# Decode attention with grouped queries: where SyncE waits for the stores of the output rows

## The chip, the cores and the metric

The kernel runs on one core of a Trainium2 chip. A core has five engines with an instruction queue each: TensorE (PE; its weight loads are listed as PEld), VectorE (DVE), ScalarE (ACT), GpSimd (POOL) and SyncE (SP), and 16 DMA engines. The engines run on their own and meet only through semaphores: an instruction may wait until a semaphore has a value and may change it when it is done. A DMA raises its semaphore by 16 in all when its data has landed. The metric is the device time of one execution, in microseconds (us); lower is better.

## What is computed

One query position attends to 65,536 keys. There are 32 query heads of 128 elements and 8 heads of keys and values, each shared by four query heads. All inputs and the output are bf16.

```
B, Hq, Hkv, Sq, Sk, D = 1, 32, 8, 1, 65536, 128

k = jnp.repeat(k, Hq // Hkv, axis=1)
v = jnp.repeat(v, Hq // Hkv, axis=1)
scores = jnp.einsum("bhqd,bhkd->bhqk", q, k) * D ** -0.5
p = softmax(scores, axis=-1)
out = jnp.einsum("bhqk,bhkd->bhqd", p, v)
```

The output is 32 rows of 128 elements, 8 KB. K and V together are 268 MB, and every element is read once.

## The kernel before

The work is cut into 16 pairs of units (two pairs for each of the 8 heads of keys). For each pair SyncE loads a part of K and of V (`load_k`, `load_v`), TensorE transposes K in blocks of 128 rows into PSUM (`trb`), VectorE and ScalarE copy the blocks to SBUF (`ktb`), and TensorE multiplies them by the four queries of the head. VectorE takes the largest score of each partition, GpSimd the largest over the partitions, ScalarE the exponentials with their sums, and TensorE multiplies the exponentials (`pts`) by V. VectorE keeps the running sum (`acc`), rescaled whenever the maximum grows.

Each engine has a function of its own (`tensor_engine`, `vector_engine`, `scalar_engine`, `gpsimd_engine`, `sync_engine`) that writes its instruction queue by hand; loops are loops on the engine. The order within a queue is the order of the source.

What stands around the change is the end of the program:

- VectorE finishes the first 28 of the 32 output rows while the last values are still being multiplied (`orow`, L378), and ScalarE stores them (L425). The last four rows, those of the last head, come last: TensorE's last products go into `acc` (L309), TensorE transposes `acc` (L208), VectorE divides by the sum of the exponentials (`olast`, L389), and SyncE stores them (L509).
- Both stores raise the same semaphore, `o_sem`, by 16 each. SyncE, whose queue ends with the second store, waits for 32 (L512).
- The five functions are given to a block (L514 to L519). When the block ends, each engine branches to its end, and there all five meet: SyncE, ScalarE, TensorE and VectorE each execute a DRAIN that raises a gather semaphore; GpSimd waits until it has four, and raises a release semaphore by four; the other four each wait for one (EVENT_SEMAPHORE) and take it. In the profile these instructions have line L520, the statement that closes the block.
- SyncE's wait for `o_sem` is not an instruction of its own in the built program: it stands on SyncE's branch to the block's end, which the profile shows as a COMPARE_BRANCH of L520.

The block at the program's start has a meeting of the same kind (L533).

Of the kernel before, what the change touches and what calls it, by code (L numbers as in the profile page):

```python
# [41 lines left out]
def take(e, sem, n=1):  # L42

    e.wait_ge(sem, n)
    e.sem_inc(sem, -n)  # L45


def bass_standalone__gqa_softmax__decode_kernel(nc, q, k, v, out):
# [14 lines left out]
    def row_tile(odd, x):  # L63
        return (x + C) % (2 * T) if odd else x
# [4 lines left out]
    S = es.enter_context  # L69
# [4 lines left out]
    def sem(name):  # L74
        return S(nc.semaphore(name))
# [48 lines left out]
    q_sem, o_sem, s_x, t_z, t_id, t_if, t_qT = (  # L124
        sem(n) for n in ("q_sem", "o_sem", "s_x", "t_z", "t_id", "t_if", "t_qT"))
# [317 lines left out]
    def pairs(x):  # L443

        return x.rearrange("h (c p t) d -> (h c) p (t d)", c=HALVES, p=P)

    def sync_engine(e):
        kp, vp = pairs(kf), pairs(vf)

        def cols(a, b):  # L450
            return slice(a * D, b * D)

        def load_k(i, odd, split=(0,)):

            for n, f in enumerate(split):
                last = (split + (len(K_PARTS),))[n + 1]
                a, b = K_PARTS[f], (K_PARTS + (2 * T,))[last]
                r = row_tile(odd, a) if b - a < 2 * T else 0
                t = r if odd else C + r
                e.dma_start(kbuf[:, cols(t, t + b - a)], kp[i][:, cols(r, r + b - a)]).then_inc(krdy[f], 16)  # L460
                for x in range(f + 1, last):
                    e.sem_inc(krdy[x], 16)

        def load_v(i, ready, a, b):
            e.dma_start(vbuf[:, cols(a, b)], vp[i][:, cols(a, b)]).then_inc(ready, 16)

        def load_both(i, odd):
            take(e, kfree)
            load_k(i, odd)
            take(e, vfree)  # L470
            load_v(i, vrdy[0], 0, 2 * T)
            e.sem_inc(vrdy[1], 16)

        load_k(0, 0, (0, 1, 2))
        load_v(0, vrdy[0], 0, 2 * T)

        for sm in [vrdy[1]] + vpiece:
            e.sem_inc(sm, 16)

        take(e, kfree)  # L480
        load_k(1, 1)
        e.wait_ge(vmid, 1)
        load_v(1, vrdy[0], C, A)
        take(e, vfree)
        e.sem_inc(vpiece[0], -16)
        load_v(1, vrdy[1], A, 2 * T)
        load_v(1, vpiece[0], 0, C)
        with e.Fori(1, H - 1) as h:
            load_both(2 * h, 0)
            load_both(2 * h + 1, 1)  # L490
        i = NR - 2
        take(e, kfree)
        load_k(i, 0, (0, 2))
        take(e, vfree)
        load_v(i, vrdy[0], 0, A)
        load_v(i, vrdy[1], A, 2 * T)
        i = NR - 1
        take(e, kfree)
        load_k(i, 1, (0, 1, 2))
        take(e, vfree)  # L500
        for sm in vpiece:
            e.sem_inc(sm, -16)
        load_v(i, vrdy[0], C, 2 * T)
        e.sem_inc(vrdy[1], 16)
        r = 0
        for n, sm in zip(V_PIECES, vpiece):
            load_v(i, sm, r, r + n)
            r += n
        ins = e.dma_start(of[HR - R:HR, :], olast[:, :])  # L509
        ins.wait_op(t_last, 1, "sem-ge")  # L510
        ins.then_inc(o_sem, 16)
        e.wait_ge(o_sem, 32)  # L512

    block = S(nc.Block())  # L514
    block.tensor(tensor_engine)
    block.vector(vector_engine)
    block.scalar(scalar_engine)
    block.gpsimd(gpsimd_engine)
    block.sync(sync_engine)  # L519
    es.close()  # L520

# [26 lines left out]
```

## Time and profile before

| | |
|---|---|
| median of 3 runs | 629.46 us |
| lowest and highest | 629.41 and 629.58 us |
| the profiled execution's own time | 629.4 us |
| its span, from the first to the last instruction of the program | 627.5 us |
| mean granted TensorE clock | 0.767 |
| HBM read | 268.44 MB, 428 GB/s over the span |

The profile is one execution. Its page lists for each engine the busy time and its share of the span, then the span in 40 slices (a digit is tenths of a slice), the DMA queues, and the chain of work that ended last. Other views list the chain in order of time, the instructions in a window (start, duration, engine, line, operation, output and inputs, and in brackets the idle time before and what ended it), the instructions of one line (durations in ns as least, median and greatest, then the first and last start in us), and who waited for whom (total, times, longest). An engine's name with a q stands for its sequencer: instructions that only wait, branch or issue a DMA, which are not counted as busy. Rows of sequencers are given to 0.1 us in these views; the trace has them in nanoseconds.

### The profile page before, as it was taken

Reading aid. Unit: us, or ns where it says so; the run is one execution under the profiler, and the core shown is the slowest. Engines: PE = TensorE matmul, PEld = TensorE weight load, DVE = VectorE, ACT = ScalarE, POOL = GpSimd, SP = SyncE. Lnnn points to the kernel's source line nnn. Section 1 sums busy time; section 2 is a strip of 40 time slices with the busy share of each in tenths; the row PEclk is TensorE's granted clock in tenths of the full one; section 3 lists DMA queues with packets and bytes.
Section 4 is the critical chain, followed back from the end, with each engine's and each line's share of the span. In section 5 each row is a group of like instructions: output and inputs, shape, how many; then the busy total and the mean of one; then the engine's idle time right before and its main releaser. Section 6 shows DMA issues by size and latency. Waiting matters only on the chain. (4 is left out here: it accounts for less than half of the span.)

```text
span 627.5 us, 26947 instructions
## 1 busy us (share of the span) xinstructions
PE 489.5 (78%) x12290; PEld 484.9 (77%) x12290; DVE 284.5 (45%) x667; ACT 235.4 (38%) x466; POOL 16.4 (3%) x49
## 2 busy tenths in 40 slices
PE   4764995949859597694977949679695894999987
PEld 4664995949859597694977949679695894999886
DVE  4340553616436164451644517245172542747364
ACT  2240442605425154350533605235152451535343
POOL 0000000000000000000000000000000000000000
PEclk9775886959768597795977959678596885969697
DMA  9999999999999999999999999999999999999997
GB/s 378 427 450 402 439 453 418 451 418 451 418 451 418 447 422 439 430 426 439 426 439 430 434 434 430 439 430 439 430 434 434 434 434 430 415 436 429 425 438 303
DMA packets 6443, 268.59 MB, mean 428 GB/s; under 512 B 802, under 2 KB 930, under 8 KB 1186
## 3 DMA queue, kind: packets, MB, share of 16 engines
q1 hardware_dynamic: 6344, 268.44, 99.2%
q8 instruction: 7, 0.11, 0.1%
q10 hardware_dynamic: 90, 0.02, 0.0%
q14 instruction: 2, 0.02, 0.0%
HBM read 268.44 MB, written 0.01 MB: 428 GB/s over the span
## 5 line engine op out<-in xcount | busy, mean ns | idle before, releaser
L139 PE MATMUL trb<-ident,kbuf 128*128 128x128 bf16 x4096 | 302.2, 237 | 108.6 <-PEq L45 102.8
L139 PEld LDWEIGHTS trb<-ident,kbuf 128*128 128x128 bf16 x4096 | 269.9, 107 | 110.3 <-issue 108.0
L233 ACT ACTIVATE ktb<-trb 128x1024 bf16<-128x1024 bf16 x176 | 180.2, 1024 | 350.2 <-PE trb L139 343.7
L235 DVE COPY ktb<-trb 128x1024 bf16<-128x1024 bf16 x336 | 221.7, 688 | 170.2 <-PE trb L139 167.0
L157 PE MATMUL qkb<-qcur,ktb 128*128 128x4 bf16 x4096 | 132.4, 164 | 0.7 <-issue 0.7
L157 PEld LDWEIGHTS qkb<-qcur,ktb 128*128 128x128 bf16 x4096 | 124.6, 96 | 0.8 <-issue 0.8
L183 PE MATMUL pvb<-pts,vbuf 128*128 128x4 bf16 x2560 | 71.7, 166 | 13.4 <-PEq L45 10.0
L183 PEld LDWEIGHTS pvb<-pts,vbuf 128*128 128x128 bf16 x2560 | 69.9, 102 | 15.2 <-issue 14.9
L403 ACT ACTIVATE pts<-qkb,negm 128x160 bf16<-128x160 f32 (+1 forms) x128 | 52.0, 549 | 0.0
L183 PE MATMUL qkb<-pts,vbuf 128*128 128x4 bf16 x1536 | 43.4, 166 | 8.1 <-PEq L45 8.1
L183 PEld LDWEIGHTS qkb<-pts,vbuf 128*128 128x128 bf16 x1536 | 42.4, 104 | 8.7 <-issue 8.6
L270 DVE TENSOR_REDUCE cmax<-qkb 128x4 f32<-128x640 f32 (+1 forms) x32 | 22.1, 691 | 59.0 <-DVEq L45 59.0
L403 ACT ACTIVATION_READ_ACCUMULATOR pts<-qkb,negm 128x1 f32 x128 | 34.2, 268 | 0.0
L439 POOL PARTITION_ALL_REDUCE cmaxa<-cmax x32 | 12.0, 375 | 576.3 <-POOLq L45 576.3
L320 DVE COPY acc<-qkb 128x4 f32<-128x4 f32 x8 | 1.3, 162 | 41.3 <-DVEq L45 41.3
L397 ACT ACTIVATE alpha<-dm 128x4 f32<-128x4 f32 x32 | 6.4, 201 | 32.1 <-ACTq L45 32.1
L298 DVE TENSOR_TENSOR lp<-lp,alpha 128x4 f32<-128x4 f32 x24 | 3.9, 163 | 26.9 <-DVEq L45 26.9
L309 DVE TENSOR_TENSOR acc<-acc,pvb 128x4 f32<-128x4 f32 x32 | 5.0, 157 | 21.0 <-DVEq L45 20.2
L287 DVE TENSOR_TENSOR m<-m,cmaxa 128x4 f32<-128x4 f32 x24 | 3.8, 159 | 8.8 <-DVEq L45 8.8
L306 DVE TENSOR_TENSOR acc<-acc,alpha 128x4 f32<-128x4 f32 x24 | 3.9, 162 | 4.2 <-DVEq L45 3.7
L288 DVE TENSOR_TENSOR dm<-m 128x4 f32<-128x4 f32 x24 | 3.9, 162 | 0.8
L299 DVE TENSOR_TENSOR lp<-lp,rsum 128x4 f32<-128x4 f32 x24 | 3.9, 161 | 0.8
(42 smaller groups left out, 30.1 us busy)
## 6 DMA issues: line engine op xcount, KB each, us to landing
kbuf<-in_k_dram SPq DMA_DIRECT2D x5, 3072.0 KB, 24.2
vbuf<-in_v_dram SPq DMA_DIRECT2D x2, 5120.0 KB, 23.2
vbuf<-in_v_dram SPq DMA_DIRECT2D x3, 3072.0 KB, 19.6
kbuf<-in_k_dram SPq DMA_DIRECT2D x1, 5120.0 KB, 17.4
kbuf<-in_k_dram SPq DMA_DIRECT2D x2, 2048.0 KB, 12.6
vbuf<-in_v_dram SPq DMA_DIRECT2D x1, 2048.0 KB, 18.0
vbuf<-in_v_dram SPq DMA_DIRECT2D x1, 1984.0 KB, 30.9
vbuf<-in_v_dram SPq DMA_DIRECT2D x1, 704.0 KB, 32.2
```

Source lines behind the costliest of these rows:

```text
L139: ins = pe.transpose(trb[j % NTB][:, i * P:(i + 1) * P], kbuf[:, t * D:(t + 1) * D], ident[:, :])
L157: ins = pe.matmul(bank[:, t * R:(t + 1) * R], lhsT=ktb[:, off:off + P], rhs=qcur[:, :], start=True, stop=True)
L183: ins = pe.matmul(vsum[q], lhsT=vbuf[:, r * D:(r + 1) * D], rhs=pts[:, r * R:(r + 1) * R], start=r == a, stop=r == b - 1)
L233: ins = e.activation(dst, trb[j % NTB][:, :], AF.Copy).then_inc(eva, 1)
L235: ins = e.tensor_copy(dst, trb[j % NTB][:, :]).then_inc(evd, 1)
L270: e.tensor_reduce(cmax[:, :], qkb[part][:, 0:n * R].rearrange("p (t g) -> p g t", g=R), AX.X, ALU.max).then_inc(cm, 1)
L288: lambda: e.tensor_tensor(dm[u % 2][:, :], mo[:, :], mn[:, :], ALU.subtract),
L298: chain(e, lambda: e.tensor_tensor(lp[:, :], lp[:, :], alpha[u % 2][:, :], ALU.mult), lambda: e.tensor_tensor(lp[:, :], lp[:, :], rsum[u % ...
L309: return lambda: e.tensor_tensor(acc, acc, vsum[q], ALU.add)
L397: e.activation(alpha[u % 2][:, :], dm[u % 2][:, :], AF.Exp, scale=scale)
L403: ins = e.activation(pv[:, g, r:r + n], sv[:, g, 0:n], AF.Exp, bias=negm[b][:, g:g + 1], scale=scale, accum_out=rsum[b][:, g:g + 1])
L439: e.partition_all_reduce(cmaxa[:, :], cmax[:, :], P, bass.bass_isa.ReduceOp.max).then_inc(cma, 1)
```

## The change

SyncE's wait for `o_sem` is taken out of its function and written behind the block, on SyncE alone. The block is opened and closed by a `with` statement of its own, where before it was closed with the tensors and semaphores by `es.close()`; the meeting's instructions have line L513 in the changed kernel and were L520 in the one before.

```diff
@@ -509,14 +509,15 @@
         ins = e.dma_start(of[HR - R:HR, :], olast[:, :])
         ins.wait_op(t_last, 1, "sem-ge")
         ins.then_inc(o_sem, 16)
-        e.wait_ge(o_sem, 32)
-
-    block = S(nc.Block())
-    block.tensor(tensor_engine)
-    block.vector(vector_engine)
-    block.scalar(scalar_engine)
-    block.gpsimd(gpsimd_engine)
-    block.sync(sync_engine)
+
+    with nc.Block() as block:
+        block.tensor(tensor_engine)
+        block.vector(vector_engine)
+        block.scalar(scalar_engine)
+        block.gpsimd(gpsimd_engine)
+        block.sync(sync_engine)
+
+    nc.sync.wait_ge(o_sem, 32)
     es.close()
```

In the built program, the five queues hold the same instructions in the same order but for two things: SyncE's branch to the block's end carries no wait, and behind SyncE's part of the meeting stands one more instruction, an EVENT_SEMAPHORE that waits for `o_sem` to reach 32 (L520 of the changed kernel). It is the last instruction of SyncE's queue; the other four engines' queues end with the meeting.

## The prediction

> **What bounds the kernel now.** I read the page first, for the span and the engines, then the chain of waits, then the last two microseconds in the timeline, the waits of SyncE, and every instruction of the meeting at the block's end (L520).
>
> ```profile
> span 627.5 us, 26947 instructions
> PE 489.5 (78%) x12290; PEld 484.9 (77%) x12290; DVE 284.5 (45%) x667; ACT 235.4 (38%) x466; POOL 16.4 (3%) x49
> DMA  9999999999999999999999999999999999999997
> q1 hardware_dynamic: 6344, 268.44, 99.2%
> ```
>
> The stream of K and V keeps the 16 DMA engines busy to the last slice (99.2% in q1), and TensorE follows it. The change touches none of this: the instructions that it moves stand after the last load on SyncE's queue. So the question is only what lies between the last store and the end, and that is read from the end of the chain and the timeline:
>
> ```profile
> 624.91 0.17 DVE acc L309
> 625.08 0.04 issue
> 625.12 0.39 PE pvb L208
> 625.50 0.03 issue
> 625.53 0.34 DVE olast L389
> ```
>
> ```profile
> 621.75 0.59 ACTq L425 DMA_DIRECT2D out_dram<-orow  x1
> ...
> 625.53 0.34 DVE L389 TENSOR_SCALAR olast<-pvb,rl 4x128 bf16<-4x128 f32 x1 [0.47 <-PE pvb L208]
> 625.89 0.35 SPq L509 DMA_DIRECT2D out_dram<-olast  x1
> ```
>
> The chain stops at olast; the last 1.6 us hold no engine work at all. They are the issue of the last store (625.89 to 626.24), its flight, and the meeting:
>
> ```profile
> SPq L520 <- DMA out_dram<-olast: 0.8, 1, 0.8
> SPq L520 <- PEq L520: 0.2, 1, 0.2
> ```
>
> ```profile
> L520 POOLq EVENT_SEMAPHORE  x2: 17/17/17, 627.3 to 627.4; - x2
> L520 POOLq DRAIN  x1: 403/403/403, 620.1 to 620.1; - x1
> L520 ACTq DRAIN  x1: 152/152/152, 622.4 to 622.4; - x1
> L520 PEldq DRAIN  x1: 425/425/425, 625.1 to 625.1; - x1
> L520 DVEq DRAIN  x1: 378/378/378, 625.5 to 625.5; - x1
> L520 SPq COMPARE_BRANCH  x1: 38/38/38, 627.1 to 627.1; - x1
> L520 SPq DRAIN  x1: 7/7/7, 627.3 to 627.3; - x1
> L520 SPq EVENT_SEMAPHORE  x1: 17/17/17, 627.4 to 627.4; - x1
> L520 ACTq EVENT_SEMAPHORE  x1: 17/17/17, 627.4 to 627.4; - x1
> L520 DVEq EVENT_SEMAPHORE  x1: 21/21/21, 627.4 to 627.4; - x1
> L520 PEldq EVENT_SEMAPHORE  x1: 51/51/51, 627.4 to 627.4; - x1
> ```
>
> SyncE waits 0.8 us for the store; that wait stands on its branch out of the block (the COMPARE_BRANCH at 627.1). The other engines drained at 620.1 to 625.9 and stand at the meeting. Only then comes SyncE's DRAIN, GpSimd gathers and releases, and all five leave at 627.4. Flight and meeting are in series. The views round these rows to 0.1 us; the trace's records have them in nanoseconds, and they also hold the updates of semaphores, which no view prints. Those that I use, in us from the span's start:
>
> ```
> SP   store L509      625.895 - 626.247
> o_sem reaches 32     627.079
> SP   branch L520     627.096 - 627.134
> SP   DRAIN           627.254 - 627.261
> POOL gather, release 627.286 - 627.303, 627.364 - 627.381
> SP, ACT, DVE, PE leave at 627.423, 627.427, 627.438, 627.469
> o_sem, first store: last update 624.733 (issue L425 ended 622.342)
> unnamed semaphore 2: 627.709 .744 .949 .993 628.016 | .114 .153 .187 .234
> cleared: numbers 207-255 from 628.163 to .254, ..., 3-53 from 628.450 to .799
> unnamed semaphore 2: 629.023 .057 .095 .139 .162 | .260 .299 .333 .379
> ```
>
> The lower half explains why the profiled execution's time is 629.40 and its span 627.47: the 1.93 us are an exit behind the program. One semaphore is passed on nine times, all others are cleared, and it is passed nine times again; the time ends 0.02 us after the last. The second round shows its hops when nobody is late: 34, 38, 44, 23, 98, 39, 34, 46 ns. In the first only the second hop differs (205 for 38): the third engine was late on its own account, by some 0.17 us. Five steps out and four back is a round trip over five engines. The clearing names them: it begins first, and with the fastest steps, in the highest block of numbers, and last, with the slowest, in the lowest. I take the ends for SyncE and TensorE (TensorE's leaving the meeting takes 51 ns, SyncE's 17), so the trip starts at TensorE and turns at SyncE, at 628.016.
>
> The Trainium skill, Runtime: NRT & Kernel Launch, section "The ~15µs preamble/postamble breakdown", describes such an exit: a barrier that goes through the five engines and back, a reset of 51 semaphores by each, a second barrier. Its sizes there (estimates 1.5, 1.5 and 2 us, in sum 5) don't fit the 1.93 us here, so the trace decides them; by either the exit comes after the last engine and its later half is the same before and after.
>
> **The change part by part.** (1) Removed: the wait on the branch. SyncE goes from the store's issue (626.247) to its DRAIN. ACT shows that step with an unconditional branch and no wait: issue L425 ends at 622.342, its DRAIN starts at 622.383, 0.04 us on, and no branch is recorded. So SyncE drains at 626.29. If the branch stays, it costs 38 ns and the 120 ns behind it that the rows above show, and the DRAIN is at 626.45. I take the first, since the branch now has no wait to carry, as ACT's hasn't.
>
> (2) Moved earlier: the meeting. From SyncE's DRAIN to TensorE's leaving it took 627.469 - 627.254 = 0.215 us. It now ends at 626.50 (626.66 with the branch), 0.97 (0.81) earlier. It lies beside the store's flight, 626.25 to 627.08, and nothing of it is on the path. GpSimd, ACT, DVE and PE have no instruction behind the meeting, so nothing of the program is queued for any of them.
>
> (3) Added: one semaphore wait on SyncE alone. It passes where the branch did, 627.096, and takes the 17 ns of SyncE's other EVENT_SEMAPHORE: 627.11. Nothing of the program is queued behind it on SyncE and no DMA is moved past it: the last store keeps its place and its wait for t_last, so 626.247 and the 0.83 us of flight stand. Span after: 627.11, that is 0.36 less.
>
> (4) Behind the span: the exit. TensorE can start the trip at 627.709 - 0.97 = 626.74, and the fourth engine can hand on at 627.993 - 0.97 = 627.02 (627.18 with the branch). SyncE turns it when it is there itself. What it needs between its last instruction and its turn is not visible, since in the profile it was there in time. Bounds: above, 628.016 - 627.423 = 0.59 us, since it was no later than that; below, 0.04, ACT's step from its store to its DRAIN. TensorE, the one engine whose start of the trip waits for no other, needs 627.709 - 627.469 = 0.24. I take 0.24, being the only such step that the trace times directly, and since SyncE's own steps (DRAIN 7 ns, leaving 17) are no slower than TensorE's. The turn is then at 627.11 + 0.24 = 627.35 and not 628.016: 0.66 us less. With 0.59 it is at 627.70, 0.31 less; with 0.04 at 627.15, 0.87 less (0.81 if the branch stays, where the other four decide).
>
> Sum against the profiled execution: 629.40 - 0.66 = 628.74; the median of the runs, 629.46, is 0.06 above it, so 628.80. Of the 0.66, 0.36 is meeting taken out of the span and 0.30 is the other four's way into the exit, which now runs while SyncE waits. The cover is the store's flight: were that nothing, the meeting would be on the path again and the change worth only the branch's 0.16.
>
> **The rivals.** *SyncE is slow into the exit* (0.59 us as the third engine must have been about: 627.381 to 627.949 if that is GpSimd): the gain is 0.31, time 629.15. For it: nothing shows SyncE earlier than 628.016. Against: its steps are the shortest of all.
>
> *The exit doesn't stand on SyncE*, or SyncE is there at once: the whole 0.81 to 0.97 of the meeting comes off, 628.49 to 628.65. Against: a trip over five engines has to pass it.
>
> *The DRAIN waits for the store itself.* Then the change does not do what it says: SyncE drains at 627.08 anyway, the meeting ends 0.215 later, at 627.30, the wait behind passes at once, and only the branch is saved: 629.40 - 0.17 + 0.06 = 629.29. Against it stands ACT: its DRAIN ended at 622.54, with the first store still in its queue:
>
> ```profile
> core 0 of [0], span 627.5 us
> q10 hardware_dynamic: 42, 0.01, 2.0%
> ```
>
> That is the DMA view of 622.54 to 624.5: all 42 packets of the first store move after ACT's DRAIN.
>
> *Slower: the store lands later, because four engines leave while it flies.* Its place is the last store, so far alone on an idle core. The price by the nearest row: the first store, beside the V stream, took 624.733 - 622.342 = 2.39 us against 0.83. With 2.39 the wait passes at 628.65, SyncE turns the trip at 628.89, 0.87 later than before: 630.33. It decides from a flight of 0.83 + 0.66 = 1.49 us on. Against: until SyncE turns the trip the four do no more than four semaphore updates (the clearing began only behind 628.016), and the store's 8 packets were through by 626.75, about when the four can begin:
>
> ```profile
> DMA packets 8, 0.00 MB, mean 1 GB/s; under 512 B 8, under 2 KB 8, under 8 KB 8
> ```
>
> (the DMA view of 626.3 to 627.0).
>
> **How the numbers follow.** Forecast 0.56, SyncE slow 0.12, not on SyncE 0.08, the DRAIN waits 0.05, slower store 0.05. The 0.14 left is for differences over the whole program that no row of the end shows: the granted clock is a mean over 627 us,
>
> ```profile
> core 0: 627.5 us, clock 0.767
> ```
>
> and a fifth of a per cent of the stream's time outweighs every case above. The predicted time is 628.8. The forecast's own range is 628.6 to 629.15; the range 628.4 to 629.5 takes in the whole meeting off (628.49) and the waiting DRAIN (629.29), each with the 0.17 that the three runs lie apart. 0.2%, about what a measurement of this kernel can tell from no change, is 1.26 us. No named case reaches it on either side, the largest gain being 0.97 and the slower one 0.87. So faster by more than that gets 0.08 and slower 0.06, both out of the unnamed part, and within it 0.86.
>
> **What would show it.** SyncE's DRAIN at about 626.3 and the four engines' leaving at about 626.5, with an EVENT_SEMAPHORE of SyncE on the new line near 627.1 as the span's end (span about 627.1). A DRAIN near 627.1 is the third rival. A DRAIN at 626.45 with a branch in front means the branch stayed. The time less the span should grow from 1.93 to about 1.63; 2.0 would be the slow SyncE, 1.4 the exit that doesn't need it. The wait passing clearly later than 0.85 us after the store's issue is the slower rival. I am wrong if anything ahead of 625.89 differs by more than runs differ: then the end is not where the time went.

## The result and the profile after

| | before | after |
|---|---|---|
| median, 22 runs each | 629.47 us | 628.62 us |
| lowest and highest | 629.28 to 629.69 | 628.48 to 628.84 |
| the profiled execution's own time | 629.4 | 628.62 |
| its span | 627.5 | 627.1 |
| ratio, 95% interval | | 0.9987 [0.9981, 0.9993] |

The changed kernel is 0.85 us faster, 0.13%: clear of the scatter of the runs (no run of one kernel reaches into the range of the other), and less than the 0.2% that the prediction took for what a measurement can tell. The page of the changed kernel shows the same stream as before:

```profile
span 627.1 us, 26947 instructions
PE 490.4 (78%) x12290; PEld 485.9 (77%) x12290; DVE 284.5 (45%) x667; ACT 235.4 (38%) x466; POOL 16.5 (3%) x49
q1 hardware_dynamic: 6344, 268.44, 99.2%
```

The busy times of the engines differ by at most 1.0 us of some 490, and the last store is issued at the same place as before, within 0.03 us. This is the end of the changed kernel's timeline (start, duration, engine, line, operation):

```profile
625.55 0.34 DVE L389 TENSOR_SCALAR olast<-pvb,rl 4x128 bf16<-4x128 f32 x1 [0.47 <-PE pvb L208]
625.92 0.35 SPq L509 DMA_DIRECT2D out_dram<-olast  x1
```

So the difference lies behind 625.92. First the waits of SyncE in the changed kernel (who waited for whom: total, times, longest), then the instructions of the meeting, now L513, and of the moved wait, now L520:

```profile
SPq L520 <- DMA out_dram<-olast: 0.5, 1, 0.5
SPq L513 <- PEq L513: 0.2, 1, 0.2
```

```profile
L513 POOLq EVENT_SEMAPHORE  x2: 17/17/17, 626.5 to 626.6; - x2
...
L513 DVEq DRAIN  x1: 380/380/380, 625.6 to 625.6; - x1
L513 SPq DRAIN  x1: 152/152/152, 626.3 to 626.3; - x1
L513 SPq EVENT_SEMAPHORE  x1: 17/17/17, 626.6 to 626.6; - x1
...
L513 PEldq EVENT_SEMAPHORE  x1: 51/51/51, 626.6 to 626.6; - x1
```

```profile
L520 SPq EVENT_SEMAPHORE  x1: 17/17/17, 627.1 to 627.1; - x1
```

SyncE is still the last to drain: its DRAIN starts at 626.3 (VectorE's at 625.6), and not at 627.3 as before, all engines have left at 626.7 and not 627.5, and what remains of the wait for the store is 0.5 us, behind the meeting. There is no COMPARE_BRANCH on SyncE any more.

For what lies behind the span I read the trace's records in nanoseconds, as in the prediction. All numbers of this table are us counted from S, the moment at which SyncE sees olast done (the start of the last store's issue; of the branch in e5 and e6; in e7, where neither is at that place, 0.027 behind olast's end, as in the others), so that the 0.3 us by which the end of the stream differs between executions drops out. Each line is one execution, the profiled one. "Turn" is the fifth update of semaphore 2, where the exit's trip over the engines turns back; "last" is its last update. The seven kernels e1 to e7 are those of the next section.

| | store landed | SyncE's DRAIN | TensorE has left | turn | last | median us |
|---|---|---|---|---|---|---|
| before | 1.184 | 1.359 | 1.574 | 2.121 | 3.484 | 629.47 |
| after | 1.185 | 0.415 | 0.775 | 1.341 | 2.686 | 628.62 |
| e1, `with` only | 1.176 | 1.350 | 1.566 | 2.112 | 3.477 | 629.45 |
| e2, wait off the branch | 1.183 | 1.275 | 1.491 | 2.038 | 3.402 | 629.39 |
| e3, GpSimd waits | 1.173 | 0.410 | 0.772 | 1.819 | 3.211 | 629.05 |
| e4, TensorE waits | 1.178 | 0.410 | 0.771 | 1.627 | 2.992 | 628.82 |
| e5, no store, form of before | none | 0.158 | 0.373 | 0.920 | 2.284 | 628.21 |
| e6, no store, changed form | none | 0.157 | 0.372 | 0.920 | 2.283 | 628.28 |
| e7, store behind the meeting | 1.423 | ahead of S | 0.243 | 1.581 | 2.924 | 628.82 |

Before to after, the turn comes 0.78 us earlier and the last update 0.80 us: that is where the time went. 0.36 of it (1.574 to 1.219, where SyncE's last instruction ends) is span; the rest is the exit behind it, 1.93 us before (629.40 - 627.47) and 1.48 after (628.62 - 627.14).

### The profile page after: what moved, and what is told of

It is laid out like the page before. It is cut to its first block, busy times and chain, and to the rows that moved or that the text cites. A ratio compares the mean times of both kernels' runs of the same rounds, so it can differ in the third digit from the quotient of the medians.

```text
span 627.1 us, 26947 instructions
## 1 busy us (share of the span) xinstructions
PE 490.4 (78%) x12290; PEld 485.9 (77%) x12290; DVE 284.5 (45%) x667; ACT 235.4 (38%) x466; POOL 16.5 (3%) x49
```

## The experiments

The theory (A): the meeting of the engines, and the way of four of them into the exit, now lie under the last store's flight, and the exit's first trip is turned by SyncE as soon as the store has landed. The rivals say that the `with` statement or the program's place in memory does it (B), the freed branch (C, D), any late engine alike (E), the other four engines' way and not SyncE's (F), or the form by itself without a flight (G). A time has an interval of about 0.1% either way in these runs, 0.6 us, so most verdicts rest on the trace's rows and not on the ratio.

**e1: only the `with` statement.**

```diff
         ins.then_inc(o_sem, 16)
+        e.wait_ge(o_sem, 32)
...
-    nc.sync.wait_ge(o_sem, 32)
     es.close()
```

> Edit: the changed kernel with the wait for o_sem back at the end of SyncE's function; the block keeps its with statement. Theory A (the gain comes from the meeting moved into the store's flight): the kernel before again, 629.47 us within 0.15, SyncE's branch waits until 627.1, the engines leave the meeting at 627.5. Rival B (the with statement, or how the program lies in memory, brings it): 628.62.

Measured: 629.45 us, ratio to the kernel before 1.0001 [0.9991, 1.001]. The rows of the meeting (L514 here) and SyncE's wait in this kernel:

```profile
SPq L514 <- DMA out_dram<-olast: 0.8, 1, 0.8
```

```profile
L514 SPq COMPARE_BRANCH  x1: 38/38/38, 627.1 to 627.1; - x1
L514 SPq DRAIN  x1: 7/7/7, 627.2 to 627.2; - x1
L514 PEldq EVENT_SEMAPHORE  x1: 51/51/51, 627.4 to 627.4; - x1
```

These rows are those of the kernel before, and in the table the columns of the trace differ from its line by at most 0.01. So the `with` statement alone does nothing. That the program's place in memory does it is answered by e6 below, which has the whole changed form without a flight and gains nothing on e5. B falls.

**e2: only the branch freed.** In the kernel before:

```diff
-        e.wait_ge(o_sem, 32)
+        take(e, o_sem, 32)
```

`take` waits and takes the 32 back, which makes the wait an instruction that doesn't go onto the branch.

> Edit: in the kernel before, the wait for o_sem is an instruction of its own (it also takes the 32 back), so that the branch to the block's end carries no wait; the meeting still stands behind the store's landing. Theory A: only the branch is saved. Wait at 627.10 to 627.11, DRAIN about 0.04 later at 627.15 where it was at 627.25, so 0.10 us less: 629.37. Rival C (most of the gain is the branch and what it fetches, and the meeting itself costs little): about 628.7. Rival D (a branch without a wait still costs its time): 629.48, DRAIN at 627.27.

Measured: 629.39 us, ratio 0.9999 [0.9989, 1.0008], which tells nothing. The rows of the wait (now on the line of `take`, the last of SyncE's 31 there) and of the meeting in this kernel:

```profile
L45 SPq EVENT_SEMAPHORE  x31: 17/17/17, 25.9 to 627.3; - x31
```

```profile
L520 SPq DRAIN  x1: 7/7/7, 627.3 to 627.3; - x1
L520 SPq EVENT_SEMAPHORE  x1: 17/17/17, 627.5 to 627.5; - x1
...
L520 PEldq EVENT_SEMAPHORE  x1: 51/51/51, 627.5 to 627.5; - x1
```

The wait ends and the DRAIN starts within the same tenth of a microsecond. The table has it finer: DRAIN at S + 1.275 for 1.359, and the last update 0.082 earlier. The branch is not recorded, and from the wait's start to the DRAIN it takes 0.077 us (627.269 to 627.346) where it took 0.158. So C falls: the branch alone is worth 0.08, a tenth of the gain. D falls too.

**e3 and e4: another engine waits.** In the changed kernel:

```diff
-    nc.sync.wait_ge(o_sem, 32)
+    nc.gpsimd.wait_ge(o_sem, 32)
```

and, for e4, `nc.tensor.wait_ge(o_sem, 32)`.

> Edit: in the changed kernel the wait behind the meeting stands on GpSimd and not on SyncE. Theory A (the exit is a trip TensorE, ACT, GpSimd, VectorE, SyncE and back, and each engine hands on when it has come into the exit on its own; GpSimd needs 0.568 us from its last instruction, in both traces: 627.381 to 627.949 and 626.607 to 627.175): wait passes at 627.12, ends 627.14, GpSimd hands on at 627.71, VectorE 0.044 and SyncE 0.023 to 0.042 later, turn at 627.78 against 627.26: 0.52 more than the changed kernel, 629.14. Rival E (only the landing and a fixed step behind it matter, whichever engine waits): 628.62. Span 627.1 by both.

> Edit: in the changed kernel the wait behind the meeting stands on TensorE and not on SyncE. Theory A: TensorE's wait passes at 627.12 and ends 0.051 later, 627.17; TensorE starts the trip 0.24 to 0.27 after it, 627.41 to 627.45, and nobody else is late by then, so hops of 34, 38, 44 and 23 ns: turn at 627.55 to 627.59 against 627.26, 0.29 to 0.33 more than the changed kernel: 628.91 to 628.95. Rival E (whichever engine waits): 628.62. Span 627.17 by both.

Measured: e3 629.05 us, ratio 0.9993 [0.9984, 1.0003]; e4 628.82, 0.9989 [0.998, 0.9999]. The last instruction of each, first of e3 and then of e4:

```profile
L520 POOLq EVENT_SEMAPHORE  x1: 17/17/17, 627.3 to 627.3; - x1
```

```profile
L520 PEldq EVENT_SEMAPHORE  x1: 51/51/51, 627.2 to 627.2; - x1
```

The first trip of semaphore 2 in the three kernels, from the trace's records:

```
after  626.969 627.003 627.175 627.219 627.261   SyncE's wait ended 627.139
e3     627.106 627.140 627.841 627.885 627.909   GpSimd's wait ended 627.303
e4     627.487 627.521 627.559 627.603 627.626   TensorE's wait ended 627.256
```

The place at which the trip is held up is that of the waiting engine: the third when GpSimd waits, the first when TensorE does, the fifth when SyncE does. This shows those three places, of which the prediction had argued the first and the last and only supposed GpSimd's. That ACT is the second and VectorE the fourth, as the expectation of e3 says, no run shows. GpSimd hands on 0.538 after its wait, TensorE 0.231, SyncE 0.122. The landing is the same in all three (S + 1.173 to 1.185), yet the last update comes 0.525 (e3) and 0.306 (e4) later than in the changed kernel, as A said (0.52, and 0.29 to 0.33). E falls.

The median times moved by less than that, 0.43 and 0.20, about 0.10 less in each. In both profiled executions the time is 0.13 us less than the last update (629.17 for 629.301; 628.86 for 628.991), while in the other kernels it is 0.01 to 0.02 more. That gap of 0.15 is large enough to account for the 0.10; where it comes from is open.

**e5 and e6: no flight.** The last store is left out of both kernels; this is e5, and e6 has the same edit in the changed kernel.

```diff
-        ins = e.dma_start(of[HR - R:HR, :], olast[:, :])
-        ins.wait_op(t_last, 1, "sem-ge")
-        ins.then_inc(o_sem, 16)
-        e.wait_ge(o_sem, 32)
+        e.wait_ge(t_last, 1)
+        e.wait_ge(o_sem, 16)
```

> Edit: the kernel before without its last store: the last four output rows (28 to 31) are not written; SyncE waits for t_last in its place, and for 16 of o_sem. The store's flight, which covers the meeting after the change, is gone. Counted from where the store would be issued (S, the moment t_last is seen): branch to S+0.04, DRAIN at S+0.16, leaving S+0.37, turn of the exit's trip 0.547 later as in the kernel before, end at S+2.28 where the kernel before ends at S+3.48: 1.20 less, 628.27.

> Edit: the changed kernel without its last store, in the same way (rows 28 to 31 are not written, SyncE's branch waits for t_last, behind the meeting it waits for 16 of o_sem, which are there). Theory A (the change pays because the meeting lies under the flight): no flight, no gain: the same as the no-store form of the kernel before within 0.1, 628.27, the turn set by GpSimd's 0.57 in the exit and not by SyncE. Rival G (an engine that waits behind the meeting is cheaper by itself, flight or no flight): some 0.8 less than that form, 627.45.

Measured: 628.21 us, ratio 0.998 [0.997, 0.999], and 628.28 us, 0.9981 [0.9971, 0.9991]. In the table the two lines agree within 0.001 us in every column of the trace, although in e6 the wait stands behind the meeting. The rows of e5 first, then those of e6 and its moved wait:

```profile
L518 SPq DRAIN  x1: 7/7/7, 625.9 to 625.9; - x1
...
L518 PEldq EVENT_SEMAPHORE  x1: 51/51/51, 626.1 to 626.1; - x1
```

```profile
L511 SPq COMPARE_BRANCH  x1: 38/38/38, 625.9 to 625.9; - x1
L511 SPq DRAIN  x1: 7/7/7, 626.1 to 626.1; - x1
...
L511 PEldq EVENT_SEMAPHORE  x1: 51/51/51, 626.3 to 626.3; - x1
```

```profile
L518 SPq EVENT_SEMAPHORE  x1: 17/17/17, 626.3 to 626.3; - x1
```

Without a flight the moved wait is worth nothing: G falls. (In both kernels the first store has landed more than 1 us ahead of S, so the wait for 16 of `o_sem` holds nothing up.) These two also bound what moving waits around the last store can gain. With no store at all the last update is at S + 2.28; the changed kernel's is at 2.69, so of the 1.20 us that the store cost before, 0.40 is left.

**e7: the store behind the meeting too.** In the changed kernel:

```diff
-        ins = e.dma_start(of[HR - R:HR, :], olast[:, :])
-        ins.wait_op(t_last, 1, "sem-ge")
-        ins.then_inc(o_sem, 16)
...
+    ins = nc.sync.dma_start(of[HR - R:HR, :], olast[:, :])
+    ins.wait_op(t_last, 1, "sem-ge")
+    ins.then_inc(o_sem, 16)
     nc.sync.wait_ge(o_sem, 32)
```

> Edit: in the changed kernel the last store itself is moved behind the meeting too, ahead of the wait for o_sem. The meeting is then released by VectorE's DRAIN (0.03 behind S, the moment t_last is seen), the engines leave at about S+0.25 instead of S+0.775, and the store is issued at S+0.25 instead of S. Theory A: the other four are 0.53 earlier in the exit and it helps nothing; SyncE's own way, store 0.25 later, sets the turn: S+1.59 against S+1.34, time 0.25 more than the changed kernel, 628.87. SyncE's DRAIN takes 7 ns, with no store in flight, where it took 152. Rival F (the other four's way into the exit is what ends last): about 0.5 less than the changed kernel, 628.1.

Measured: 628.82 us, ratio to the kernel before 0.999 [0.998, 1.0]. The meeting (L510), the wait behind it and the store in this kernel:

```profile
L510 SPq DRAIN  x1: 122/122/122, 593.0 to 593.0; - x1
...
L510 DVEq DRAIN  x1: 378/378/378, 625.5 to 625.5; - x1
L510 SPq EVENT_SEMAPHORE  x1: 17/17/17, 626.1 to 626.1; - x1
...
L510 PEldq EVENT_SEMAPHORE  x1: 51/51/51, 626.1 to 626.1; - x1
```

```profile
626.14 0.35 SPq L517 DMA_DIRECT2D out_dram<-olast  x1
```

```profile
L520 SPq EVENT_SEMAPHORE  x1: 17/17/17, 627.3 to 627.3; - x1
```

SyncE has drained at 593.0 already, all leave at 626.1, 0.53 earlier than in the changed kernel, and the store starts 0.245 later. The first four updates of the trip come at 626.382 to 626.666; the fifth comes only at 627.480, 0.124 after SyncE's wait. The last update is 0.24 later than the changed kernel's, the median 0.20 (expected 0.25). SyncE's step from its wait to the turn is the same as in the changed kernel (0.122), although there the other four were 0.53 later. So what ends last in the changed kernel is SyncE's own way, if only by 0.02 us (see below), and F falls. One part of the expectation was wrong: the DRAIN took 122 ns and not 7; it came 0.057 us behind the issue of the last load of V.

## Why the prediction was right, point by point

**Nothing ahead of the store moves.** Right: the store starts at 625.92 for 625.89, and its flight is 0.833 us for 0.832 (issue's end to the 32nd count of o_sem).

**The removed wait on the branch.** Right: no branch is recorded, and the DRAIN starts 0.06 behind the issue (0.04 forecast). Its share alone is 0.08 (e2), half of the 0.16 that it was given, because the wait itself and the way to the DRAIN still take 0.077.

**The moved meeting.** Right in place, off in size: the engines leave at 626.70 and not 626.50. The prediction took the meeting's 0.215 us over as it was, but SyncE's DRAIN, 7 ns in the kernel before, takes 152 with the store just issued. It cost nothing, being under the flight. But the forecast left the other four 0.33 us of margin (627.02 against SyncE's 627.35), and hardly any of it is left: the fourth engine hands on at 627.219, 0.042 before SyncE, where the hop alone takes 0.023. The two ways into the exit are level within 0.02 us, so hiding more of the meeting gains no more than that.

**The added wait.** Right: it passes at 627.122, ends at 627.139, and the span is 0.33 less (0.36 counted from S, as forecast).

**The exit.** This is the term that was mis-sized. "What it needs between its last instruction and its turn" was bounded by 0.04 and 0.59 and taken as 0.24, from TensorE's step. It is 0.122 in the changed kernel and 0.124 in e7. In the traces, counted from S, the last update came 0.80 earlier where 0.66 was forecast: 0.12 of the 0.14 is this term, and 0.02 lies behind the turn (1.345 us from the turn to the last update, before 1.363). The medians differ by another 0.05 (0.85), less than the 0.17 by which the first three runs of the kernel before lie apart. The exit fell from 1.93 us to 1.48 (the prediction's text says "grow", its numbers mean a fall), between the 1.63 forecast and the 1.4 of the rival in which it does not stand on SyncE.

**The range.** 628.62 lies at the lower edge of the forecast's own range (628.6 to 629.15) and inside that of a rival, so the time alone does not tell them apart; the rows do. The lower end of the wide range does not follow as it is told: 628.49 less 0.17 is 628.32, not 628.4.

**The rivals.** SyncE slow into the exit: no, 0.12; the slow one is GpSimd (0.57 in both traces). The exit not standing on SyncE: its time, 628.49 to 628.65, came true and its mechanism did not, as the trip in e7 stops 0.8 us at SyncE. The second half of that rival, "or SyncE is there at once", was nearly true: SyncE holds the trip up by only 0.02 us. The DRAIN waiting for the store: no; it ended at 626.487, 0.62 before the landing. The store slowed by the engines that leave: no; 0.833 us.

The exit's description in the Trainium skill, Runtime: NRT & Kernel Launch, section "The ~15µs preamble/postamble breakdown", tells of a barrier that passes through the engines in turn, and in this e3, e4 and e7 agree with it. Its 1.5 us for the first barrier does not fit: from the end of the last instruction to the trip's last update it is 0.77 us in the kernel before (627.469 to 628.234). The trip itself takes 0.53 of that, of which 0.17 is GpSimd's lateness.

A kernel that doesn't wait for the last store at all was not tried, since nothing in the program would then order the store before its end. In the changed kernel it is ordered: the store has landed at 627.105, and the semaphores are cleared only from 627.411 on.

## What to carry to other kernels

A wait that nothing but the program's end needs can stand behind the last meeting of the engines, on one engine; what it then saves is the part of the meeting and of the other engines' way out that the flight covers: here 0.80 us under a flight of 0.83, and nothing without one (other lengths of flight were not tried). Of the three engines tried, SyncE was the best place, the one that the exit reaches last and that was quickest into it: the same wait moved the last update by 0.31 us more on TensorE and 0.53 more on GpSimd (the median by 0.20 and 0.43). ACT and VectorE were not tried. And look behind the span: less than half of this gain lay inside it.

## What the hardware showed that was not expected

- SyncE's DRAIN takes 7 ns when its last DMA was issued 0.9 us before or longer (before, e1, e2, e5, e6) and 122 to 153 ns within 0.07 us of an issue (after, e3, e4, e7), without waiting for the data: in the changed kernel it ended 0.62 us ahead of the landing. Which of the two, the time since the issue or the landing, makes it short again is open.
- The engines need different times from their last instruction to their hand-on in the exit: SyncE 0.12 us, TensorE 0.23 to 0.27, GpSimd 0.54 to 0.57. ACT's and VectorE's were not separated.
- A wait that stands on a branch costs 0.158 us to the next instruction, the same wait as an instruction of its own 0.077.
